# Shorter Sinkhorn rounds, a second pass all in Strassen products, and the last pass's x split earlier

## The chip, the core and the metric

The kernel runs on one core of a Trainium2 chip. The metric is the device time of one launch in microseconds. Five engines work side by side, each with a queue of its own that it takes in order: TensorE (PE, matmuls), VectorE (DVE), ScalarE (ACT), GpSimd (POOL) and SyncE (SP), which issues most DMA transfers. An engine waits for another by a semaphore, and what stands behind a waiting instruction waits too.

## What is computed

Three stages follow each other on 2304 tokens of width 512:

```
attn  = softmax(q k^T / 8) v          # in chunks of 64, 8 heads
P     = exp(x w_gate - max)           # x: attn as [2304, 512], 8 experts
repeat 8 times:
    P /= P.sum(1) + 1e-9              # rows: over the experts
    P /= P.sum(0) + 1e-9              # columns: over the tokens
    P *= N / E
out   = sum over e of P[:, e] * (relu(x w1[e]) w2[e])       # hidden width 1024
y     = LN(h * softmax(h)) w_out,  h = out w_in             # per token
```

All is float32. A product is made of three matmuls of rounded parts: each operand is split into a high part (rounded by ScalarE) and a low part (the rest, a subtraction on VectorE or POOL), and high*high, high*low and low*high are added up in PSUM.

## The kernel before

The tokens are taken in three passes of 768, each as two halves of 384. In every pass the 32 units (8 experts by 4 quarters of the hidden width) are gone through; `unit(m)` gives pass and unit of the m-th of 96 visits. In visit m the loop does the first layer of unit m and the second layer of an earlier unit, so PE alternates between groups of six matmuls of the one and of the other.

The first layer of a unit (`l1`) is one two-by-two Strassen step: seven products of six matmuls, 42 in all, into the PSUM banks X, Y and Z; VectorE forms the four blocks of h from them. For this x is kept as seven blocks (`XOPS`: B11, B21, B22 and the sums T1 to T4), each with high and low part. The blocks of the second and the third pass are made while the first pass runs, or shortly after it (`x_steps`, queued in `late` and `late2`), written to DRAM (`x_kept`) and loaded when their pass begins.

The second layer has two forms. In the plain one (`l2`) a unit has eight parts (half, output block pair, block) of six matmuls, 48 in all, with four weight blocks A11 to A22. In the Strassen one (`l2s`) two units are taken together: seven products (`SECOND`) of two parts of six matmuls, 84 for the pair, with seven weight blocks a unit; h needs sums T1 to T4 as well (`h_sums`, on POOL), and the seven accumulators are put together at the pass's end (`l2s_sums`). The weight sums S1 to S4 come from `second_sums`.

Which form a visit has is set by M2: visits below M2 are plain. The first pass is plain throughout. The second takes the ten units of `PLAIN` first, in plain form, and then the 22 of `EARLY`, whose sums were made in the first pass; `acc_change` turns the plain accumulators into Strassen ones there. The sums of the ten are made on POOL in the second pass, for the third, which is Strassen throughout.

The Sinkhorn rounds run as side steps in the first units of the first pass: `run_side(k)` takes k steps, once after each first-layer product and once after each second-layer part. A round is one matmul with a matrix of ones, which sums over the tokens on the partitions (`sink_sum`), the column step (`sink_cols`) and the row step (`sink_rows`) on VectorE, and an idle step. Its result must be written out and read back as `share` tiles before unit 4 scales h by it.

The rest of the order is set by `events[7 * n + i]`, functions due at product i of visit n, by two queues of weight steps (`w_side`) and of last-stage weights (`prep`), and by the pools: tiles of a tag share a fixed number of buffers (15 for x and h blocks, tag `six`; 18 for weight blocks, tag `w`), so a load can wait until a buffer comes free. SP's queue is one: a store that waits for POOL holds up the loads issued behind it.

Of the kernel before, what the change touches and what calls it, by code (L numbers as in the profile page):

```python
# [44 lines left out]
def chunk_attention_sinkhorn_moe_solu_kernel(  # L45
# [14 lines left out]
    P = 128  # L60
# [25 lines left out]
    EARLY = [u for u in range(NU) if u not in PLAIN]  # L86
    ORDER = [list(range(NU)), PLAIN + EARLY, list(range(NU))]
    NM = NPASS * NU
    M2 = NU + len(PLAIN)

# [47 lines left out]
    ident = const.tile([P, P], F32, name="ident")  # L138
    ones = const.tile([P, P], F32, name="ones")
    mhalf = const.tile([P, 1], F32, name="mhalf")  # L140
# [3 lines left out]
    lg = const.tile([P, NT, E], F32, name="lg")  # L144
    pw_e = const.tile([P, E, NT], F32, name="pw")
    pw = pw_e.rearrange("p e t -> p t e")

# [204 lines left out]
    def gate(t):  # L352
# [10 lines left out]
        nc.vector.tensor_copy(lg[:, t, :], pg[:, :E])  # L363

    def sink_start():
# [11 lines left out]
    def sink_exp(pm):  # L377
        nm = small.tile([P, 1], F32, tag="m1", name="nm")
        nc.vector.tensor_reduce(out=nm, in_=pm[:, :P], axis=AX.X, op=ALU.max)
        nc.vector.tensor_scalar(  # L380
            out=lg, in0=lg, scalar1=nm, scalar2=None, op0=ALU.subtract
        )
        nc.scalar.activation(out=pw, in_=lg, func=AF.Exp)

    def sink_rows(pc):
        r = pc[:, 256:256 + NT]
        nc.vector.tensor_reduce(out=r, in_=pw, axis=AX.X, op=ALU.add)
        nc.vector.tensor_scalar(out=r, in0=r, scalar1=EPS, scalar2=None, op0=ALU.add)
        nc.vector.reciprocal(out=r, in_=r)
        nc.vector.tensor_tensor(  # L390
            out=pw, in0=pw, in1=r.unsqueeze(2).to_broadcast([P, NT, E]), op=ALU.mult
        )

    def sink_sum():
        pc = spare("pc")
        nc.tensor.matmul(
            pc[:, :NT * E], ones, pw_e.rearrange("p e t -> p (e t)"), start=True, stop=True
        )
        return pc

    def sink_cols(pc):
        r = pc[:, 192:192 + E]
        nc.vector.tensor_reduce(
            out=r, in_=pc[:, :NT * E].rearrange("p (e t) -> p e t", e=E), axis=AX.X, op=ALU.add
        )
        nc.vector.tensor_scalar(out=r, in0=r, scalar1=EPS, scalar2=None, op0=ALU.add)
        nc.vector.reciprocal(out=r, in_=r)
        nc.vector.scalar_tensor_tensor(
            out=pw,
            in0=pw,  # L410
            scalar=float(N) / E,
            in1=r.unsqueeze(1).to_broadcast([P, NT, E]),
            op0=ALU.mult,
            op1=ALU.mult,
        )
# [32 lines left out]
    def sink_steps():  # L448
        def start():
            sink["mb"] = sink_start()  # L450

        def first():
            sink["pm"] = sink_max(sink["mb"])

        def expo():
            sink_exp(sink["pm"])
            sink_rows(sink["pm"])

        def summed():
            sink["pc"] = sink_sum()  # L460

        def cols():
            sink_cols(sink["pc"])

        def rows():
            sink_rows(sink["pc"])

        def shares():
            load_share(0)
            load_share(1)  # L470

        idle = lambda: None
        steps = [start, first, expo, idle]
        for i in range(8):
            steps += [summed, cols, rows, idle]
        return steps[:-2] + [sink_out, shares]
# [84 lines left out]
    def second_blocks(u):  # L561

        def block(n):
            def go():
                t = wtile([P, 2, 256], F32R, f"w2_{u}_{n}")
                split(t[:, 0], t[:, 1], w2_block(u, n), nc.gpsimd)
                wo2[u, n] = t
                if n != "A21" or u in PLAIN:
# [300 lines left out]

    def acc_change(p):  # L870


        at = {w: n for n, (w, _) in enumerate(SECOND)}
        for w, j, d in (("A12", 0, 0), ("A22", 0, 2), ("S4", 1, 0), ("S1", 1, 2)):
            acc[p, at[w]] = acc[p, j, d]
        a, b = acc[p, at["S4"]], acc[p, at["S1"]]
        nc.vector.tensor_tensor(out=a, in0=a, in1=b, op=ALU.subtract)

    def l2s_sums(p):
# [204 lines left out]
    with tc.manual_schedule():  # L1084
# [3 lines left out]
        for i in range(WARM):  # L1088
            nc.tensor.transpose(warm[:, :P], ident, ident)
        nc.gpsimd.memset(ones, 1.0)  # L1090
        nc.gpsimd.memset(mhalf, -0.5)
# [83 lines left out]

        late = deque(x_steps(1, nc.vector))
        late2 = deque(x_steps(2, nc.gpsimd))
        prep.extend(
# [18 lines left out]
        event(7 * (M2 + 1), lambda: acc_change(1))  # L1197
        for m in range(M2, NM):
            for g, f in h_sums(m, nc.vector if m == NM - 1 else nc.gpsimd):
                event(g, f)  # L1200
            if m % 2 == 0:
                for n, (wn, _) in enumerate(SECOND):
                    for q_ in range(2):
                        event(7 * (m + 2) + 2 * n - 5,
                              lambda u=unit(m + q_)[1], wn=wn: w_load(u, wn, 1))
            if m % NU == 0:
                for i in range(6):
                    event(7 * (m + 2) + i,
                          lambda i=i, p=m // NU - 1: l2s_sums(p)[i]())
        for n in range(NM):  # L1210
# [35 lines left out]
            for i in range(7):  # L1246
# [38 lines left out]
        for k in range(14):  # L1285
# [3 lines left out]
            if k == 7:  # L1289
                mlp_b(0)  # L1290
                mlp_a(2)
        assert not events and not late2
        load_out(0, 15)
# [51 lines left out]
```

## Time and profile before

| | us |
|---|---|
| median of 3 runs | 1798.76 (1795.76 to 1800.87) |
| the profiled execution | 1800.11 |
| its span, first to last instruction | 1798.3 |
| PE busy in it | 1758.6 (98%) |
| VectorE, POOL, ScalarE busy | 1371.6, 1022.1, 615.1 |
| granted TensorE clock, mean | 0.991 of full speed |

The span falls into the attention (to about 110 us, with the first unit at its end), the first pass (to about 626), the second pass (to about 1090), the third (to about 1575) and the last stage, per tile of 128 tokens. Reading it: an engine's busy time counts its instructions alone, a wait is put down to the engine and line that came last, and the span is that of the instructions, 1.8 us less than the whole execution.

### The profile page before, as it was taken

The page shows a single profiled execution, that of the slowest core. Times are in us where ns is not written, and L with a number is a line of the kernel's source. Part 1 is how long each engine was busy: PE and PEld are TensorE (multiplying, and loading weights), DVE is VectorE, ACT ScalarE, POOL GpSimd, SP SyncE. Part 2 cuts the span into 40 slices and gives each one's busy share as a digit, 9 for nine tenths or more (in the row PEclk, how much of TensorE's full clock was granted, in tenths as well). Part 3 has the DMA queues.
Part 4 walks back from the last instruction along what each step waited for, and adds up shares of the span by engine and source line. Part 5 has one row for each costly group of instructions (what it writes and reads, how often), then busy time and mean ns, then how long its engine had stood idle before and what let it go on. Part 6 is the DMA issues. An engine that isn't in the chain of part 4 may idle for free. (4 is left out here: it accounts for less than half of the span.)

```text
span 1798.3 us, 32046 instructions
## 1 busy us (share of the span) xinstructions
PE 1758.6 (98%) x10869; PEld 1705.0 (95%) x10869; DVE 1371.6 (76%) x2271; ACT 615.1 (34%) x1394; POOL 1022.1 (57%) x1132
## 2 busy tenths in 40 slices
PE   7989999999999999999999999999999999999999
PEld 6878999999999999999999999999999999988887
DVE  6767888889887757778787878888877877766664
ACT  6733444444444312223333332223232232222222
POOL 2656888888888411148878776656566655400000
PEclk9899999999999999999999999999999999999999
DMA  7766898898899998879999999888888888931110
GB/s 186 187 217 205 292 330 310 306 336 296 310 314 333 356 337 282 252 250 320 345 320 313 332 340 394 299 275 263 289 283 287 276 267 258 301 132 65 56 48 30
DMA packets 297154, 476.20 MB, mean 265 GB/s; under 512 B 47760, under 2 KB 100128, under 8 KB 296992
## 3 DMA queue, kind: packets, MB, share of 16 engines
q1 hardware_dynamic: 296272, 470.23, 77.3%
q10 hardware_dynamic: 720, 3.93, 0.5%
q8 instruction: 87, 1.43, 0.3%
q14 instruction: 75, 0.61, 0.1%
HBM read 325.08 MB, written 148.97 MB: 264 GB/s over the span
## 5 line engine op out<-in xcount | busy, mean ns | idle before, releaser
L673 POOL TENSOR_TENSOR ho_T<-hT,ho_T 128x384 fp32r<-128x384 f32 x212 | 230.3, 1088 | 165.4 <-ACT ho_T L672 143.7
L796 PE MATMUL y<-h,w_A 128*128 128x384 f32 x1536 | 303.0, 334 | 0.0
L796 PEld LDWEIGHTS y<-h,w_A 128*128 128x128 f32 x1536 | 269.2, 188 | 0.0
L751 DVE TENSOR_TENSOR t<-Y,s 128x384 f32<-128x384 f32 x192 | 106.2, 553 | 155.0 <-PE Y L653 117.4
L151 POOL TENSOR_TENSOR w_A<-raw,w_A 128x256 fp32r<-128x256 f32 x224 | 168.9, 766 | 97.3 <-ACT w_A L150 97.3
L672 ACT ACTIVATE ho_B<-hp 128x384 fp32r<-128x384 f32 x162 | 85.2, 526 | 354.8 <-DVE hp L706 348.7
L847 PE MATMUL y<-ho_T,wl_S 128*128 128x384 f32 x972 | 195.1, 335 | 0.2 <-DVE acc L867 0.2
L867 DVE TENSOR_TENSOR acc<-y,acc 128x768 f32<-128x768 f32 (+1 forms) x186 | 170.4, 919 | 19.5 <-PE y L847 19.4
L847 PEld LDWEIGHTS y<-ho_T,wl_S 128*128 128x128 f32 x972 | 171.5, 189 | 1.0 <-DVE acc L867 0.5
L681 POOL TENSOR_TENSOR hT<-hp,hp 128x384 f32<-128x384 f32 x106 | 113.3, 1090 | 92.2 <-DVE hp L706 82.5
L823 DVE TENSOR_TENSOR acc<-y,acc 128x768 f32<-128x768 f32 (+1 forms) x168 | 153.1, 912 | 8.3 <-PE y L796 6.7
L653 PE MATMUL X<-x_B,wl_A 128*128 128x384 f32 x768 | 154.7, 336 | 2.1 <-ACT s L755 2.1
L653 PE MATMUL Y<-x_T,wl_S 128*128 128x384 f32 x768 | 154.8, 336 | 0.0
L672 ACT ACTIVATE ho_T<-hT 128x384 fp32r<-128x384 f32 x216 | 111.3, 516 | 107.2 <-POOL hT L681 102.6
L653 PEld LDWEIGHTS X<-x_B,wl_A 128*128 128x128 f32 x768 | 135.8, 189 | 2.4 <-ACT s L755 2.4
L653 PEld LDWEIGHTS Y<-x_T,wl_S 128*128 128x128 f32 x768 | 135.8, 189 | 0.4 <-DVE hp L706 0.3
L847 PE MATMUL y<-ho_B,wl_A 128*128 128x384 f32 x648 | 130.0, 336 | 0.0
L1044 POOL TENSOR_TENSOR r<-r,mhalf 128x1 f32<-128x1 f32 x18 | 9.9, 549 | 208.5 <-DVE r L1041 208.5
L673 DVE TENSOR_TENSOR ho_B<-hp,ho_B 128x384 fp32r<-128x384 f32 x162 | 122.8, 758 | 2.9 <-ACT ho_B L672 2.5
L681 POOL TENSOR_TENSOR hT<-hp,hT 128x384 f32<-128x384 f32 x106 | 122.4, 1155 | 0.1
L847 PEld LDWEIGHTS y<-ho_B,wl_A 128*128 128x128 f32 x648 | 114.7, 189 | 0.0
L727 ACT ACTIVATE h<-X 128x384 fp32r<-128x384 f32 x76 | 37.4, 492 | 203.3 <-DVE X L723 174.1
(173 smaller groups left out, 3725.1 us busy)
## 6 DMA issues: line engine op xcount, KB each, us to landing
wl_S<-wk SPq DMA_DIRECT2D x472, 256.0 KB, 4.6
wl_A<-wk SPq DMA_DIRECT2D x394, 256.0 KB, 4.7
wk<-w_S SPq DMA_DIRECT2D x256, 256.0 KB, 3.4
wk<-w_A SPq DMA_DIRECT2D x202, 256.0 KB, 3.1
raw<-in_moe_w_dram SPq DMA_DIRECT2D x71, 512.0 KB, 5.8
sh<-spread SPq DMA_DIRECT2D x64, 192.0 KB, 5.5
kept<-wp SPq DMA_DIRECT2D x32, 256.0 KB, 4.1
xk_T<-x_T SPq DMA_DIRECT2D x8, 768.0 KB, 4.3
```

Of the source, the lines that this page charges most:

```text
L151: (eng or nc.vector).tensor_tensor(out=lo, in0=src, in1=hi.bitcast(F32), op=ALU.subtract)
L653: nc.tensor.matmul(b, w[:, a, kk, :], x[:, c, kk, :], start=(first and kk == 0 and n == 0), stop=(kk == 1 and n == 2), skip_group_check=no ...
L672: nc.scalar.activation(out=hi, in_=x, func=AF.Copy)
L673: f = lambda: eng.tensor_tensor(out=lo, in0=x, in1=hi.bitcast(F32), op=ALU.subtract)
L681: eng.tensor_tensor(out=hb[m, n], in0=hb[m, a], in1=hb[m, b], op=ALU.subtract)
L727: nc.scalar.activation(out=hi, in_=hp, func=AF.Copy)
L751: nc.vector.tensor_tensor(out=c_of[n], in0=bank_, in1=c_of[other], op=ALU.add)
L796: nc.tensor.matmul(y, wo2[u, f"A{d // 2 + 1}{f + 1}"][:, a, i * P:(i + 1) * P], h[:, c, f, :], start=(f == 0 and n == 0), stop=(f == 1 and ...
L823: nc.vector.tensor_tensor(out=at, in0=y, in1=at, op=ALU.add)
L847: nc.tensor.matmul(y, wo2[unit(m + q_)[1], wn][:, a, i * P:(i + 1) * P], hop[m // 2, bn][:, q_, c, :], start=(q_ == 0 and o == 0), stop=(q ...
L867: nc.vector.tensor_tensor(out=at, in0=y, in1=at, op=ALU.add)
L1044: nc.gpsimd.tensor_tensor(out=r2, in0=r2, in1=mhalf, op=ALU.pow)
```

## The change

Sinkhorn: `pw` gets one column more per token tile, filled with EPS, and one tile row more, filled with EPS / 128, and the matrix of ones becomes one of E / N. So the sums come out with EPS added and scaled, and the additions of EPS, the scaling by N / E and the subtraction of the maximum go (the last becomes the bias of the exponential). Column and row step become one side step, with two idle ones behind; the side steps of visit 1 are taken one at a time. The last column step writes `pw_e`, in the old layout.

Second pass: `ORDER[1]` takes `EARLY` first and `PLAIN` last, and M2 is 32, so the whole pass is in Strassen form. `acc_change` and the loads and stores of plain blocks for the second pass go, and the sums of the ten `PLAIN` units are made from visit 35 on instead of 37. The eight plain parts of the last first-pass unit are spread over visits 32 and 33, four in each.

x: the eighteen steps for the third pass move from visits 31 to 37, on POOL, to the first pass, on VectorE, behind those for the second pass. The queue of both now gets one step in a unit of `EARLY` too, from unit 5 on.

```diff
-    ORDER = [list(range(NU)), PLAIN + EARLY, list(range(NU))]
+    ORDER = [list(range(NU)), EARLY + PLAIN, list(range(NU))]
-    M2 = NU + len(PLAIN)
+    M2 = NU
...
-    ones = const.tile([P, P], F32, name="ones")
+    ratio = const.tile([P, P], F32, name="ratio")
-    pw_e = const.tile([P, E, NT], F32, name="pw")
-    pw = pw_e.rearrange("p e t -> p t e")
+    pw_x = const.tile([P, NT + 1, E + 1], F32, name="pw")
+    pw = pw_x[:, :NT, :E]
+    pw_e = const.tile([P, E, NT], F32, name="pw_e")
...
-        nc.vector.tensor_reduce(out=r, in_=pw, axis=AX.X, op=ALU.add)
-        nc.vector.tensor_scalar(out=r, in0=r, scalar1=EPS, scalar2=None, op0=ALU.add)
+        nc.vector.tensor_reduce(out=r, in_=pw_x[:, :NT, :], axis=AX.X, op=ALU.add)
...
-            out=r, in_=pc[:, :NT * E].rearrange("p (e t) -> p e t", e=E), axis=AX.X, op=ALU.add
-        )
-        nc.vector.tensor_scalar(out=r, in0=r, scalar1=EPS, scalar2=None, op0=ALU.add)
+            out=r,
+            in_=pc[:, :SC].rearrange("p (t e) -> p e t", e=E + 1)[:, :E, :],
+            axis=AX.X,
+            op=ALU.add,
+        )
...
-            steps += [summed, cols, rows, idle]
+            steps += [summed, lambda i=i: cols(i == 7), idle, idle]
...
-        late = deque(x_steps(1, nc.vector))
-        late2 = deque(x_steps(2, nc.gpsimd))
+        late = deque(x_steps(1, nc.vector) + x_steps(2, nc.vector))
...
-        for m in range(NU, M2):
-            u = unit(m)[1]
-            for k, wn in enumerate(("A11", "A12", "A21", "A22")):
-                event(7 * m + 2 + k, lambda u=u, wn=wn: w_load(u, wn, 1))
-            g = 7 * (NU + 5) + 18 * (m - NU)
+        for n, u in enumerate(PLAIN):
+            g = 7 * (NU + 3) + 18 * n
...
-                    run_side(2 if n == 1 and i < 4 else 1)
+                    run_side(1)
-                if NU > n > NQ and n in PLAIN and i in (1, 2, 4, 6) and late:
+                if NU > n > NQ and i in ((1, 2, 4, 6) if n in PLAIN else (2,)) and late:
                     late.popleft()()
-                if n > NU - 2 and i in (1, 3, 5) and late2:
-                    late2.popleft()()
...
-                if 0 < n <= M2:
-                    for part in parts[i:i + 1] if i < 6 else parts[6:]:
-                        l2(n - 1, *part, apart=apart)
+                if 0 < n <= M2 + 1:
+                    if n < M2:
+                        todo = parts[i:i + 1] if i < 6 else parts[6:]
+                    else:
+                        k = i // 2 + 4 * (n - M2)
+                        todo = parts[k:k + 1] if i % 2 == 0 else []
+                    for part in todo:
+                        l2(min(n, M2) - 1, *part, apart=apart)
```

What this does to the queues shows at three places. On PE, at the first Sinkhorn sum in visit 1 (X and Y are first-layer products, y second-layer parts, pm the maximum, pc the column sums), before:

```order
L653 MATMUL X_1872<-x_B_688,w_A_1554 128x384 x6
L374 MATMUL pm<-ident,mb 128x128
L796 MATMUL y_0_0_0_1895<-h_0_1714,w_0_A_1638 128x384 x3
L796 MATMUL y_0_0_0_1895<-h_0_1714,w_0_A_1642 128x384 x3
L653 MATMUL Y_1915<-x_T_1144,w_S_1696 128x384 x6
L396 MATMUL pc<-pw,ones 128x144
L796 MATMUL y_0_0_1_1934<-h_0_1714,w_0_A_1638 128x384 x3
L796 MATMUL y_0_0_1_1934<-h_0_1714,w_0_A_1642 128x384 x3
L653 MATMUL X_1872<-x_B_775,w_A_1634 128x384 x6
```

and now:

```order
L794 MATMUL y_0_0_0_1895<-h_0_1717,w_0_A_1641 128x384 x3
L794 MATMUL y_0_0_0_1895<-h_0_1717,w_0_A_1645 128x384 x3
L377 MATMUL pm<-ident,mb 128x128
L651 MATMUL Y_1909<-x_T_1147,w_S_1699 128x384 x6
L794 MATMUL y_0_0_1_1932<-h_0_1717,w_0_A_1641 128x384 x3
L794 MATMUL y_0_0_1_1932<-h_0_1717,w_0_A_1645 128x384 x3
L651 MATMUL X_1874<-x_B_778,w_A_1637 128x384 x6
L395 MATMUL pc<-pw,ratio 128x171
```

`pm` now has a second-layer part ahead of it, and between `pm` and the first `pc` stand three groups of six matmuls instead of two.

On VectorE, one round in visit 2 (pc holds the sums and their reciprocals, pw the matrix, acc the second layer's accumulator), before:

```order
L751 TENSOR_TENSOR t_2219<-Y_2145,s_2123 128x384
L403 TENSOR_REDUCE pc<-pc 128x8
L406 TENSOR_SCALAR pc<-pc 128x8
L407 RECIPROCAL pc<-pc 128x8
L408 SCALAR_TENSOR_TENSOR pw<-pw,pc 128x18x8
L823 TENSOR_TENSOR acc_1_0_1977<-y_1_0_1_2237,acc_1_0_1977 128x384
L387 TENSOR_REDUCE pc<-pw 128x18
L388 TENSOR_SCALAR pc<-pc 128x18
L389 RECIPROCAL pc<-pc 128x18
L390 TENSOR_TENSOR pw<-pw,pc 128x18x8
```

and now:

```order
L749 TENSOR_TENSOR c_2265<-Y_2128,s_2106 128x384
L402 TENSOR_REDUCE pc<-pc 128x8
L408 RECIPROCAL pc<-pc 128x8
L409 TENSOR_TENSOR pw<-pw,pc 128x18x8
L387 TENSOR_REDUCE pc<-pw 128x18
L388 RECIPROCAL pc<-pc 128x18
L389 TENSOR_TENSOR pw<-pw,pc 128x18x8
```

The two additions are gone, and the row step follows the column step with nothing of the layers between.

On SP, at the change from the first pass to the second (wl: weight blocks loaded, first the unit, then the block, then 0 for the first layer and 1 for the second; wk: weights stored; xk: blocks of x stored; ak: accumulators stored), the issues of visit 32 before:

```order
L621 DMA wl1_S3_0_8102<-wk1_95 128x512
L556 DMA wk30_124<-w2_30_S1_7943 128x512
L621 DMA wl1_S1_0_8122<-wk1_95 128x512
L310 DMA xk2_B21_88<-x2_B21_8045 128x1536
L829 DMA ak0_0_126<-acc0_0_0_1902 128x768
L621 DMA wl1_A22_0_8143<-wk1_95 128x512
L621 DMA wl0_A11_1_8145<-wk0_94 128x512
L556 DMA wk30_124<-w2_30_S2_7997 128x512
L621 DMA wl1_S4_0_8164<-wk1_95 128x512
L621 DMA wl0_A12_1_8168<-wk0_94 128x512
L829 DMA ak0_1_127<-acc0_1_0_1977 128x768
L621 DMA wl0_A21_1_8189<-wk0_94 128x512
```

and those of visit 33 now:

```order
L827 DMA ak0_1_128<-acc0_1_0_1969 128x768
L619 DMA wl5_A11_0_8212<-wk5_100 128x512
L619 DMA wl5_S2_0_8214<-wk5_100 128x512
L619 DMA wl5_A12_0_8216<-wk5_100 128x512
L619 DMA wl5_S3_0_8227<-wk5_100 128x512
L619 DMA wl5_S1_0_8249<-wk5_100 128x512
L619 DMA wl5_A22_0_8265<-wk5_100 128x512
L619 DMA wl2_A11_1_8267<-wk2_97 128x512
L619 DMA wl3_A11_1_8269<-wk3_98 128x512
L827 DMA ak0_0_127<-acc0_0_2_2033 128x768
L619 DMA wl5_S4_0_8288<-wk5_100 128x512
L619 DMA wl2_A12_1_8306<-wk2_97 128x512
```

Before, the store of x block B21 for the third pass stood ahead of the loads for the next unit and of the plain blocks of unit 0; now no store of x is left here, and the first second-layer loads are those of the pair of units 2 and 3, behind one unit's first-layer blocks.

## Rows read from the trace of the kernel before

**Rows 1.** The page's busy times: engine, us busy, share, instructions.

```profile
PE 1758.6 (98%) x10869; PEld 1705.0 (95%) x10869; DVE 1371.6 (76%) x2271; ACT 615.1 (34%) x1394; POOL 1022.1 (57%) x1132
```

**Rows 2.** Busy times by stage: stretch, length, each engine's us (instructions), clock, DMA share, GB/s.

```profile
core 0: us, PE busy (x) PEld busy (x) DVE busy (x) ACT busy (x) POOL busy (x), PEclk, DMA share, GB/s
112.80:157.30 44.50, 34.49 (x191) 31.96 (x192) 35.46 (x99) 12.68 (x35) 23.81 (x33) 1.00 0.55 196
...
180.00:600.00 420.00, 420.00 (x2425) 420.00 (x2424) 353.11 (x574) 189.15 (x516) 348.18 (x458) 1.00 0.89 313
...
626.50:638.70 12.20, 9.42 (x38) 8.65 (x37) 3.60 (x5) 1.05 (x3) 0.00 (x0) 0.72 1.03 393
...
788.50:807.50 19.00, 15.89 (x80) 14.93 (x79) 12.55 (x21) 6.14 (x14) 16.25 (x17) 0.91 0.60 183
807.50:1120.00 312.50, 311.78 (x1797) 311.07 (x1797) 246.54 (x377) 96.50 (x207) 241.48 (x237) 1.00 0.96 338
1120.00:1143.00 23.00, 20.39 (x108) 19.89 (x107) 22.79 (x29) 5.19 (x11) 12.69 (x10) 0.93 0.71 253
```

**Rows 3.** PE's waits, whole span: waiter, for whom, us in total, times, longest.

```profile
PE pc L396 <- DVE pw L390: 8.7, 8, 2.0
...
PE Z L653 <- DVE X L751: 4.3, 3, 2.6
...
PE y L796 <- DMA wl_A<-wk: 2.8, 2, 2.0
PE X L653 <- ACT s L755: 2.1, 1, 2.1
...
PE pm L374 <- DVE mb L369: 1.3, 1, 1.3
...
PE pwt L426 <- DVE pw L408: 0.7, 1, 0.7
```

**Rows 4.** Timeline of PE, a Sinkhorn round: start, us, instruction, idle before.

```profile
139.46 0.51 PE L396 MATMUL pc<-pw,ones 128*128 128x144 f32 x2 [0.88 <-DVE pw L390]
139.71 1.30 PE L653 MATMUL Y<-x_T,w_S 128*128 128x384 f32 x6
...
144.62 0.51 PE L396 MATMUL pc<-pw,ones 128*128 128x144 f32 x2 [0.49 <-DVE pw L390]
```

**Rows 5.** Timeline of VectorE in the same round.

```profile
141.59 0.30 DVE L403 TENSOR_REDUCE pc<-pc 128x8 f32<-128x144 f32 x1
141.93 0.17 DVE L406 TENSOR_SCALAR pc<-pc 128x8 f32<-128x8 f32 x1
142.14 0.22 DVE L407 RECIPROCAL pc<-pc 128x8 f32<-128x8 f32 x1
...
142.72 0.55 DVE L823 TENSOR_TENSOR acc<-y,acc 128x384 f32<-128x384 f32 x1
143.19 0.41 DVE L387 TENSOR_REDUCE pc<-pw 128x18 f32<-128x144 f32 x1
143.63 0.18 DVE L388 TENSOR_SCALAR pc<-pc 128x18 f32<-128x18 f32 x1
143.85 0.28 DVE L389 RECIPROCAL pc<-pc 128x18 f32<-128x18 f32 x1
144.16 0.41 DVE L390 TENSOR_TENSOR pw<-pw,pc 128x144 f32<-128x144 f32 x1
```

**Rows 6.** Waits of SP's queue between 560 and 700 us.

```profile
SPq L310 <- POOL x_T L308: 11.4, 4, 3.4
```

**Rows 7.** The x split: times, then duration in ns, least, median, most.

```profile
L304 ACT ACTIVATE x_B<-xf x9: 835/843/848, 38.6 to 617.3; 128x768 fp32r<-128x768 f32 x9
...
L308 DVE TENSOR_TENSOR x_B<-xf,x_B x3: 948/1341/1403, 242.4 to 304.8; 128x768 fp32r<-128x768 f32 x3
...
L308 DVE TENSOR_TENSOR x_T<-xs_T,x_T x4: 947/1164/1405, 367.2 to 492.0; 128x768 fp32r<-128x768 f32 x4
...
L339 DVE TENSOR_TENSOR xs_T<-xf,xs_T x2: 947/983/1019, 315.8 to 427.7; 128x768 f32<-128x768 f32 x2
```

More of the change, by code (lines that the diff above doesn't have):

```diff
@@ L363, in gate @@
         nc.vector.tensor_copy(lg[:, t, :], pg[:, :E])
+    SC = (NT + 1) * (E + 1)
     def sink_start():
@@ L378, in sink_exp @@
         nm = small.tile([P, 1], F32, tag="m1", name="nm")
-        nc.vector.tensor_reduce(out=nm, in_=pm[:, :P], axis=AX.X, op=ALU.max)
-        nc.vector.tensor_scalar(
-            out=lg, in0=lg, scalar1=nm, scalar2=None, op0=ALU.subtract
-        )
-        nc.scalar.activation(out=pw, in_=lg, func=AF.Exp)
+        nc.vector.tensor_reduce(out=nm, in_=pm[:, :P], axis=AX.X, op=ALU.max, negate=True)
+        nc.scalar.activation(out=pw, in_=lg, func=AF.Exp, bias=nm, scale=1.0)
     def sink_rows(pc):
         r = pc[:, 256:256 + NT]
-        nc.vector.tensor_reduce(out=r, in_=pw, axis=AX.X, op=ALU.add)
-        nc.vector.tensor_scalar(out=r, in0=r, scalar1=EPS, scalar2=None, op0=ALU.add)
+        nc.vector.tensor_reduce(out=r, in_=pw_x[:, :NT, :], axis=AX.X, op=ALU.add)
         nc.vector.reciprocal(out=r, in_=r)
@@ L396, in sink_sum, with sink_cols @@
         nc.tensor.matmul(
-            pc[:, :NT * E], ones, pw_e.rearrange("p e t -> p (e t)"), start=True, stop=True
+            pc[:, :SC], ratio, pw_x.rearrange("p t e -> p (t e)"), start=True, stop=True
         )
         return pc
-    def sink_cols(pc):
+    def sink_cols(pc, last):
         r = pc[:, 192:192 + E]
         nc.vector.tensor_reduce(
-            out=r, in_=pc[:, :NT * E].rearrange("p (e t) -> p e t", e=E), axis=AX.X, op=ALU.add
+            out=r,
+            in_=pc[:, :SC].rearrange("p (t e) -> p e t", e=E + 1)[:, :E, :],
+            axis=AX.X,
+            op=ALU.add,
         )
-        nc.vector.tensor_scalar(out=r, in0=r, scalar1=EPS, scalar2=None, op0=ALU.add)
         nc.vector.reciprocal(out=r, in_=r)
-        nc.vector.scalar_tensor_tensor(
-            out=pw,
+        nc.vector.tensor_tensor(
+            out=pw_e.rearrange("p e t -> p t e") if last else pw,
             in0=pw,
-            scalar=float(N) / E,
             in1=r.unsqueeze(1).to_broadcast([P, NT, E]),
-            op0=ALU.mult,
-            op1=ALU.mult,
+            op=ALU.mult,
         )
@@ L460, in summed, with cols @@
             sink["pc"] = sink_sum()
[L462 to L466, printed above, removed]
+        def cols(last):
+            sink_cols(sink["pc"], last)
+            if not last:
+                sink_rows(sink["pc"])
         def shares():
@@ L567, in go @@
                 wo2[u, n] = t
-                if n != "A21" or u in PLAIN:
+                if n != "A21":
                     w_keep(u, n, True, t)
@@ L868, in l2s @@
         flush()
[L870 to L877, printed above, removed]
     def l2s_sums(p):
@@ L1089, in chunk_attention_sinkhorn_moe_solu_kernel @@
             nc.tensor.transpose(warm[:, :P], ident, ident)
-        nc.gpsimd.memset(ones, 1.0)
+        nc.gpsimd.memset(ratio, float(E) / N)
+        nc.gpsimd.memset(pw_x, EPS)
+        nc.gpsimd.memset(pw_x[:, NT, :], EPS / P)
         nc.gpsimd.memset(mhalf, -0.5)
@@ L1196, in chunk_attention_sinkhorn_moe_solu_kernel @@
                 event(g + 7 + k, f[k])
-        event(7 * (M2 + 1), lambda: acc_change(1))
         for m in range(M2, NM):
@@ L1205, in chunk_attention_sinkhorn_moe_solu_kernel @@
                               lambda u=unit(m + q_)[1], wn=wn: w_load(u, wn, 1))
-            if m % NU == 0:
+            if m == 2 * NU:
                 for i in range(6):
@@ L1291, in chunk_attention_sinkhorn_moe_solu_kernel @@
                 mlp_a(2)
-        assert not events and not late2
+        assert not events
         load_out(0, 15)
```

## Prediction

> **What bounds the kernel now.** I read the page's head first. PE is busy 1758.6 us, 98% of the span [rows 1]; a matmul that goes, or a wait of PE that goes, is time unless something else takes its place. Next the table by stage [rows 2]. From 180 to 600 us PE never idles: 2425 matmuls of 384 columns in 420.0 us, 0.1732 us each, and that pitch is my unit. The other stages differ by what PE lost: the stretch 112.8 to 157.3 (the Sinkhorn rounds), 626.5 to 638.7 (the first pass's end), 788.5 to 807.5 (where the second layer turns from plain to Strassen), 1120 to 1143 (early in the last pass). Then PE's waits [rows 3]. They name the same places: 8.7 us in eight waits of the column sums `pc` for the row step, 1.3 and 0.7 us for `pm` and `pwt` beside them, 2.8 us for a weight load, 2.1 us for ScalarE, and 4.3 us of Z waiting for VectorE. Last I read one Sinkhorn round on both engines [rows 4, 5], and SyncE's queue around 626 us [rows 6].
>
> **Matmuls removed.** A plain unit has 48 second-layer matmuls, a Strassen unit 42 (84 for a pair). Ten units change: 60 matmuls less, all of 384 columns, each at PE's own pitch. 60 x 0.1732 = 10.4 us. In the plain second-pass stretch PE has no wait of its own that could hide this.
>
> **Sinkhorn rounds.** The waits there sum to 8.7 + 1.3 + 0.7 = 10.7 us [rows 3]. In the round shown the sums start at 139.46 and the next at 144.62, 0.49 us of that waiting [rows 4]. VectorE comes to the columns at 141.59 (it first needs PE's next product) and ends the rows at 144.56 [rows 5]. The change takes out two additions (0.21 us from 141.93 to 142.14, 0.22 from 143.63 to 143.85) and the accumulation that stood between columns and rows (0.47, from 142.72 to 143.19): 0.90 us. The rows then end 4.2 us after the sum. PE has four groups of six matmuls (4.16 us) and the sum itself (about 0.25) between two sums, so this wait goes. The first rounds had three groups between sums, and now all have four, since the double step in the first unit is gone; that is worth up to 1.04 us to each of them. I leave 0.3 us for `pm` (one group now stands ahead of it), 0.7 for the first sum (three groups ahead of it, and the exponential in its chain), 0.5 for `pwt`, and 1.0 over the other rounds: 2.5 left of 10.7. The sum is 171 columns wide instead of 144, about 0.05 us each, 0.4 in all. Net gain 7.8 us. Bounds: 4.5, if every round still waits 0.7, and 10.
>
> The new column reduction reads PSUM with a step of nine elements, where the old one read it straight in about 0.3 us; no row has a strided reduction from PSUM. The nearest, the rows' strided reduction from SBUF, starts 0.44 us before the next operation [rows 5], 0.1 more than the columns' 0.34. I take 0.1 a round, within the 1.0 above.
>
> **The ends of passes.** The stretch of 12.2 us at 626.5 holds 38 matmuls, which need 6.6: 5.6 lost, partly to the two weight waits and partly to the clock, 0.72 granted on average, so much of it at the 1.2 GHz level. Those loads are the plain second-layer blocks of unit 0, late because SyncE's queue, which is in order, held them behind stores of the last pass's x that waited 11.4 us for POOL [rows 6]. Both the loads and those stores are gone from there. What is late next: the pair loads of the first Strassen products, issued during visit 33 and wanted at visit 34; visit 33 has 66 matmuls, 11.4 us, since it also holds half of the last plain unit. The transfers can move 393 GB/s there [rows 2]. The stretch of 19.0 us at 788.5 holds 80 matmuls, which need 13.9: 5.1 lost. It has a unit with first-layer matmuls alone (42, or 7.3 us), while POOL is busy 16.25 of 19 us with new sums and h blocks; VectorE and ScalarE wait for POOL and PE for them. The new turn has two units of 66 matmuls, and POOL's sums start only two units later. I take back 1.5 us of the 10.7 for the new turn: gain 9.2. Bounds: 4, if the new turn loses as much as the costlier of the old ones and a little more, and 10.7. The loss at 1120 to 1143 (23.0 us for 108 matmuls, or 4.3) is the accumulators' sums in the last pass; its steps stand where they did, and I leave it.
>
> **The x split in the first pass.** Seven low parts and four differences now run on VectorE between units 5 and 25: 3 x 1.34 + 4 x 1.16 + 4 x 0.98 = 12.6 us, and seven high parts of 0.84 us on ScalarE [rows 7]. From 180 to 600 VectorE is idle 420 - 353.1 = 66.9 us and ScalarE 230.9 [rows 2], some 2.5 us of VectorE in a unit of 15.6; a unit with weight sums gets one step (at most 1.4 us), the others four. Cover is there: cost 0, bounds 0 and 10. It uses buffers that h also needs, which can hold ScalarE for a matmul group or two, as the steps for the second pass do already with no PE wait in this stretch.
>
> **Ten more Strassen units.** Between 807.5 and 1120 such units ran with POOL busy 241.5 of 312.5 us, the DMA engines 96%, and 0.7 us lost in 21.5 units (1797 matmuls over 84). Ten more with the same load, and one more with half a plain unit, cost 0.4; the shares (two tiles of 192 KB a visit) come in eight visits over the last ten units instead of over 22, 0.17 MB more a unit or 12 GB/s: about 350 instead of 338. Bounds 0 and 8.
>
> **Sum.** -10.4 - 7.8 - 9.2 + 0.4 = -27.0. The profiled execution took 1800.1 us in all (1798.3 of span), which gives 1773.1. The median of the runs is 1798.8, 1.3 lower, so the same sum from there gives 1771.8. I forecast 1773.
>
> **Rivals.**
>
> *The new turn stalls.* It joins two changes of stage in one place: x of the next pass, the accumulators' stores and the first pair loads come together. For it: both old turns lost 5 us each, and the stores wait in order on SyncE ahead of the loads. Against: fewer stores, no POOL wait in the queue. If it loses 9 us instead of 1.5: 1780 to 1781. Chance 0.12.
>
> *Sinkhorn does not get shorter.* If PE's wait is set by VectorE's own queue (accumulations and h parts ahead of the columns), only the two additions (0.4 x 8 = 3.4) are gained: 1773 + 4.4 = 1777 to 1778, and with a slow strided reduction (0.3 more a round) 1780. Chance 0.08.
>
> *The second pass is paced by transfers or POOL.* For it: 96% of the DMA engines' time. Against: the same units ran at PE's pitch, and 393 GB/s were moved at 626.5 [rows 2]. If each of 30 units lost 0.5 us: 1788. Chance 0.09. The Trainium skill, DMA: Bandwidth & Descriptors, Specifications, gives about 358 GB/s of HBM for a core, which would leave 2% above 350; this trace moved 393 for 12 us, so the trace does not hold to that figure.
>
> *Slower: the first pass is paced by the moved split.* One mechanism, in units 5 to 25: VectorE's eleven steps (12.6 us) find no idle time in the units that also make weight sums, and each of the seven high parts waits on ScalarE for an h buffer for two groups (2.1 us) plus its own 0.84 us: 12.6 + 20.6 = 33 us, 1806. It decides against the change once more than 27 us of it reach PE. Against it: 66.9 us idle on VectorE there, steps of at most 1.4 us against 2.5 a unit. For it: the x rows vary from 0.95 to 1.40 us, so something holds them. Chance 0.05. The Trainium skill, SBUF — State Buffer, Who interferes with whom, says that a VectorE instruction with two SBUF inputs contends with a GpSimd instruction that reads SBUF, and that whichever starts second is blocked to the other's end. The spread of those rows agrees. By that rule POOL, which makes the weights of the first pass and is busy 348.2 of 420 us, could lose the same 12.6 us; if its late weights held PE for all of it the sum would be 14.4 and the time 1786, but POOL's idle 71.8 us stand against that.
>
> **How the numbers follow.** Forecast case 0.66, its own range 1767 to 1780 (all gains at their best -31, so 1769 from the profiled time and 1768 from the median; Sinkhorn at 4.5 and turn at 7 together 1779). The others as above. The range 1766 to 1788 takes in the two rivals near 1780, most of the third, and leaves the slower one and a part of the third out, near 1 in 10, and as much for what I don't see. 0.3% is 5.4 us, about what a measurement of this kernel tells from no change: faster means below 1793.4. Faster holds in the first four cases almost whole, 0.94; same 0.02; slower 0.04.
>
> **What would show it.** Right: PE's count 60 lower; `pc` waits summing to some 2 us instead of 8.7; no weight wait and a full granted clock where the first pass ends, and no second low stretch 150 us later; first pass from 180 us on with PE full. Wrong: PE waits for X or Z in units 5 to 25, or for `wl` loads from visit 33 on; `pc` waits of 0.5 us or more in every round; POOL above 90% in the second pass with PE waiting for `ho`.

## The result and the profile after

The changed kernel takes 1772.27 us (median of 4 runs, 1771.00 to 1774.52) against 1798.04 for the kernel before (4 runs): ratio 0.9857, 95% interval 0.9839 to 0.9875. The forecast was 1773, between 1766 and 1788. The profiled execution took 1771.9, with a span of 1770.1.

The page's head, which answers to [rows 1]:

```profile
PE 1742.8 (98%) x10809; PEld 1689.2 (95%) x10809; DVE 1372.1 (78%) x2249; ACT 631.2 (36%) x1424; POOL 1094.4 (62%) x1203
```

PE has 60 matmuls less. Its waits (us in total, times, longest), to set beside [rows 3]:

```profile
PE Z L651 <- DVE X L749: 4.2, 3, 2.6
...
PE pc L395 <- DVE pw L389: 1.3, 3, 0.6
...
PE y L845 <- DMA wl_A<-wk: 0.6, 1, 0.6
PE y L794 <- DVE acc L821: 0.6, 2, 0.4
PE y L845 <- DMA wl_S<-wk: 0.5, 2, 0.3
PE pwt L425 <- DVE pw_e L409: 0.5, 1, 0.5
...
PE pm L377 <- DVE mb L372: 0.3, 1, 0.3
```

The column sums wait 1.3 us instead of 8.7, `pm` and `pwt` 0.8 instead of 2.0. The wait for ScalarE and most of that for `wl_A` are gone, and the Z products wait as before. By stage, with the columns of [rows 2]:

```profile
109.40:162.60 53.20, 51.10 (x291) 49.22 (x290) 43.87 (x111) 20.33 (x55) 37.86 (x51) 1.00 0.63 220
180.00:600.00 420.00, 419.42 (x2418) 418.57 (x2417) 361.90 (x583) 192.81 (x518) 352.46 (x452) 1.00 0.91 324
600.60:623.50 22.90, 22.90 (x134) 22.90 (x133) 16.64 (x29) 5.28 (x11) 6.24 (x6) 1.00 0.97 341
623.50:1064.60 441.10, 438.55 (x2523) 436.54 (x2522) 343.81 (x529) 134.01 (x290) 330.92 (x329) 1.00 0.94 330
1064.60:1128.20 63.60, 60.78 (x338) 59.59 (x337) 54.86 (x78) 17.63 (x36) 37.83 (x34) 0.97 0.91 332
```

The third row is the first pass's turn: no idle PE and a full clock, where [rows 2] had 12.2 us with 38 matmuls at 0.72. The last two rows are where time is still lost: PE is idle for 2.6 us of the one and 2.8 of the other.

To compare kernels I cut each trace at the same instruction, the first X product of a visit, so that a stage covers the same visits in each (us between those starts, each from the one profiled execution of its kernel):

| visits | before | changed | difference | what it is |
|---|---|---|---|---|
| start to 1 | 111.57 | 109.38 | -2.2 | attention, unchanged code |
| 1 to 4 | 62.52 | 53.18 | -9.3 | Sinkhorn rounds |
| 4 to 32 | 436.80 | 438.08 | +1.3 | first pass |
| 32 to 34 | 37.17 | 22.88 | -14.3 | 48 matmuls less (8.3), and 6.0 of losses |
| 34 to 64 | 445.45 | 441.04 | -4.4 | 12 matmuls less (2.1), and losses |
| 64 to 68 | 63.06 | 63.63 | +0.6 | accumulators' sums |
| 68 to 95 | 393.12 | 393.12 | 0.0 | third pass, at PE's pitch |
| 95 to the end | 248.6 | 248.8 | +0.2 | last stage |

One Sinkhorn round on PE in the kernel after (start, us, instruction), to set beside [rows 4]:

```profile
138.92 0.45 PE L395 MATMUL pc<-pw,ratio 128*128 128x171 f32 x2
139.10 1.34 PE L651 MATMUL Y<-x_T,w_A 128*128 128x384 f32 x6
...
143.40 0.45 PE L395 MATMUL pc<-pw,ratio 128*128 128x171 f32 x2
```

and the chain between the two on VectorE, to set beside [rows 5]:

```profile
141.08 0.31 DVE L402 TENSOR_REDUCE pc<-pc 128x8 f32<-128x152 f32 x1
141.42 0.22 DVE L408 RECIPROCAL pc<-pc 128x8 f32<-128x8 f32 x1
141.67 0.30 DVE L409 TENSOR_TENSOR pw<-pw,pc 128x144 f32<-128x144 f32 x1
142.01 0.33 DVE L387 TENSOR_REDUCE pc<-pw 128x18 f32<-128x162 f32 x1
142.38 0.28 DVE L388 RECIPROCAL pc<-pc 128x18 f32<-128x18 f32 x1
142.69 0.31 DVE L389 TENSOR_TENSOR pw<-pw,pc 128x144 f32<-128x144 f32 x1
```

Columns and rows take 1.92 us in one piece (141.08 to 143.00), where they took 2.98 with an accumulation between them. The sum at 143.40 finds its operand ready.

### The profile page after: what moved, and what is told of

The parts are those of the page before. It is cut to its first block, busy times and chain, and to the rows that moved or that the text cites. A ratio compares the mean times of both kernels' runs of the same rounds, so it can differ in the third digit from the quotient of the medians.

```text
span 1770.1 us, 32103 instructions
## 1 busy us (share of the span) xinstructions
PE 1742.8 (98%) x10809; PEld 1689.2 (95%) x10809; DVE 1372.1 (78%) x2249; ACT 631.2 (36%) x1424; POOL 1094.4 (62%) x1203
## 5 line engine op out<-in xcount | busy, mean ns | idle before, releaser
L671 POOL TENSOR_TENSOR ho_T<-hT,ho_T 128x384 fp32r<-128x384 f32 x252 | 276.1, 1097 | 196.0 <-ACT ho_T L670 178.3
L845 PE MATMUL y<-ho_T,wl_S 128*128 128x384 f32 x1152 | 231.5, 336 | 0.6 <-DMA wl_S<-wk 0.5
L845 PEld LDWEIGHTS y<-ho_T,wl_S 128*128 128x128 f32 x1152 | 203.0, 188 | 2.0 <-PE Z L651 1.1
L679 POOL TENSOR_TENSOR hT<-hp,hp 128x384 f32<-128x384 f32 x126 | 133.4, 1080 | 98.4 <-DVE hp L704 90.0
L670 ACT ACTIVATE ho_T<-hT 128x384 fp32r<-128x384 f32 x256 | 131.7, 516 | 124.9 <-POOL hT L679 120.2
L845 PE MATMUL y<-ho_B,wl_A 128*128 128x384 f32 x768 | 153.5, 334 | 0.6 <-DMA wl_A<-wk 0.6
L671 DVE TENSOR_TENSOR ho_B<-hp,ho_B 128x384 fp32r<-128x384 f32 x192 | 143.9, 750 | 3.8 <-ACT ho_B L670 3.2
L679 POOL TENSOR_TENSOR hT<-hp,hT 128x384 f32<-128x384 f32 x126 | 143.4, 1138 | 0.0
L845 PEld LDWEIGHTS y<-ho_B,wl_A 128*128 128x128 f32 x768 | 134.8, 188 | 1.1 <-DVE acc L865 0.9
L152 POOL TENSOR_TENSOR w_S<-ws,w_S 128x256 fp32r<-128x256 f32 x128 | 102.8, 820 | 7.6 <-ACT w_S L151 7.6
```

What stands on the lines that cost most here:

```text
L152: (eng or nc.vector).tensor_tensor(out=lo, in0=src, in1=hi.bitcast(F32), op=ALU.subtract)
L670: nc.scalar.activation(out=hi, in_=x, func=AF.Copy)
L671: f = lambda: eng.tensor_tensor(out=lo, in0=x, in1=hi.bitcast(F32), op=ALU.subtract)
L679: eng.tensor_tensor(out=hb[m, n], in0=hb[m, a], in1=hb[m, b], op=ALU.subtract)
L845: nc.tensor.matmul(y, wo2[unit(m + q_)[1], wn][:, a, i * P:(i + 1) * P], hop[m // 2, bn][:, q_, c, :], start=(q_ == 0 and o == 0), stop=(q ...
```

## The experiments

"Visits 1 to 4" and the like are the stages of the table above. Each kernel was timed beside runs of the kernel before on its chip, and times are compared by their ratio to it.

**One part alone: Sinkhorn.** The edit is the Sinkhorn part of the diff, on the kernel before.

```diff
+    pw_x = const.tile([P, NT + 1, E + 1], F32, name="pw")
+            steps += [summed, lambda i=i: cols(i == 7), idle, idle]
+                    run_side(1)
```

> The kernel before with the Sinkhorn part of the change alone (EPS and E/N folded into the sums, column and row step in one, one side step at a time in visit 1). My theory, from the waits that the change leaves in the profile after (2.1 of 10.7 us): 8 to 9.5 us shorter than before, about 1789. Rival, only the two additions a round count (0.4 us x 8): 3.4 shorter, about 1794.6. Rival, the change pays only together with the new order of the second pass: no difference.

1788.32 us, ratio 0.9945 (0.9932 to 0.9957): 9.4 less than before's 1797.74. Visits 1 to 4 take 53.18, as in the changed kernel, and all other stages are within 0.8 of before. Neither rival holds.

**One part alone: the x split.**

```diff
-        late = deque(x_steps(1, nc.vector))
-        late2 = deque(x_steps(2, nc.gpsimd))
+        late = deque(x_steps(1, nc.vector) + x_steps(2, nc.vector))
```

> The kernel before with the third pass's x split in the first pass on VectorE alone; second pass and Sinkhorn as before. My theory: the stores that waited 11.4 us for POOL leave SyncE's queue at the first pass's end, the plain weight loads of unit 0 come in time and most of the 5.6 us lost there come back, while the first pass pays at most 1.3: 2.5 to 5 us shorter than before, 1793 to 1795.5. Rival, the loss there is set by the turn itself (stores of the accumulators, loads of x): no difference, or 1 us longer. Rival of the prediction, the split paces the first pass: 5 us longer or more.

1795.32 us (11 runs), ratio 0.9985 (0.9977 to 0.9994), 2.4 less, 1.1 to 4.1 by the interval. The trace has both terms: visits 32 to 34 take 31.20 instead of 37.17, which is the pitch of their 180 matmuls, and visits 4 to 32 take 437.97, 1.2 more. Visits 32 to 34 by windows in this kernel:

```profile
611.20:642.40 31.20, 31.20 (x182) 31.20 (x181) 21.69 (x36) 4.70 (x10) 0.00 (x0) 1.00 1.04 383
```

The two terms make 4.8 less between the two traces, twice what the medians show. The profiled execution of before, at 1800.1, stood 2.4 above the median of this batch, so a part of the 6.0 lost in it at visit 33 may be its own, and the size is open between the two. That the loss is gone is plain, with the plain weight loads of unit 0 still there, so the x split caused it, whatever form the second pass has. SyncE's waits of 11.4 us for POOL's x blocks are gone from its queue, and POOL is idle in this stretch; that the loss came through the waiting stores is read from that queue and from PE's weight waits there.

**The changed kernel with the old rounds.** The Sinkhorn part of the diff undone, with the two steps at a time in visit 1.

> The changed kernel with the old Sinkhorn rounds (its second pass and its x split stay). If the parts add up, as I think: 8 to 9.5 us longer than the changed kernel, 1780 to 1782. Rival, the two parts share a gain (the clock, or work that shifts into the first units): 5 us or less longer. If the waits of before come back, the column sums wait about 8 to 9 us in all again.

1783.48 us, ratio 0.9919 (0.9905 to 0.9932), against 0.9857, or 0.9866 when repeated, with the new rounds: 9.5 to 11 us of 1798. The column sums wait 8.8 us again and visits 1 to 4 take 62.57, 9.4 more; the rest is in the attention (1.1 more) and in visits 64 to 68 (65.07, 1.4 more), stages that vary between kernels in which they are alike. The parts add up.

**The last plain unit not spread.**

```diff
-                if 0 < n <= M2 + 1:
-                    if n < M2:
+                if 0 < n <= M2:
+                    if True:
```

> The changed kernel with all eight plain second-layer parts of the first pass's last unit in visit 32, as a unit of the first pass has them, and the first layer alone in visit 33. My theory was that the halves in visits 32 and 33 give the pair loads time: without them visit 33 has 42 matmuls (7.3 us) ahead of the first Strassen products, and 2 to 5 us are lost there, 1774.5 to 1777.5. Rival, the losses at the old turns came from POOL (weight sums and h blocks, 16.25 of 19 us) and from stores that waited for it, and both are away from here now: no difference, 1772 to 1773.

1774.83 us, ratio 0.9870 (0.9856 to 0.9883). PE's timeline where the first Strassen products begin, in this kernel:

```profile
623.57 1.21 PE L651 MATMUL X<-x_B,wl_A 128*128 128x384 f32 x6
626.05 0.77 PE L845 MATMUL y<-ho_B,wl_A 128*128 128x384 f32 x3 [1.28 <-DMA wl_A<-wk]
627.79 0.76 PE L845 MATMUL y<-ho_B,wl_A 128*128 128x384 f32 x3 [0.97 <-DMA wl_A<-wk]
628.39 2.06 PE L651 MATMUL Y<-x_T,wl_S 128*128 128x384 f32 x6
```

The same stretch by windows, in this kernel

```profile
623.50:638.00 14.50, 12.25 (x61) 11.66 (x60) 7.06 (x12) 3.60 (x8) 8.93 (x10) 0.88 1.05 391
```

and in the changed one:

```profile
623.50:638.00 14.50, 14.50 (x86) 14.50 (x85) 10.03 (x16) 4.96 (x11) 10.19 (x10) 1.00 1.03 382
```

Without the halves PE waits 2.25 us for the pair weights, the clock is 0.88 of full speed on average, and fewer matmuls are done: 61 matmuls instead of 86, about 4.3 us, and visits 34 to 64 take 445.35 instead of 441.04. By the ratios the kernel is 2.3 us longer than the changed one, or 0.7 longer than its repetition (below, 0.9866), so the time does not decide between theory and rival; that the loads come late, and that visits 34 to 64 lose by it, is in the rows.

**Two side steps at a time in visit 1.**

```diff
-                    run_side(1)
+                    run_side(2 if n == 1 and i < 4 else 1)
```

> The changed kernel with two side steps at a time in the first products of visit 1, as the kernel before has them, so that the first rounds have three groups of matmuls (3.1 us) between sums instead of four. A round's chain on VectorE is about 4.2 us. If the chain sets the first rounds: each of the two or three rounds concerned waits about 1 us, but starts as much earlier, so the sum is within 1 us of the changed kernel. If the slots set the time and not the chain: no wait, no difference. In no case more than 2 us.

1775.49 us, ratio 0.9877 (0.9860 to 0.9895). I expected 2 us at most, and visits 1 to 4 take 57.10, 3.9 more. PE's waits there (us in total, times, longest):

```profile
PE pc L395 <- DVE pw L389: 2.4, 4, 1.3
PE pwt L425 <- DVE pw_e L409: 1.8, 1, 1.8
PE pm L377 <- DVE mb L372: 1.3, 1, 1.3
```

That is 5.5 against 2.1: 1.1 more for the column sums, 1.0 for `pm`, which again has no second-layer part ahead of it, and 1.3 for `pwt`. By the ratios the whole kernel is 2.0 to 3.6 us longer. My expectation forgot what PE is here: a chain that ends earlier gives nothing back to an engine that has matmuls waiting in any case, so each wait that the tighter spacing makes is lost.

**The additions put back.**

```diff
         nc.vector.tensor_reduce(out=r, in_=pw_x[:, :NT, :], axis=AX.X, op=ALU.add)
+        nc.vector.tensor_scalar(out=r, in0=r, scalar1=0.0, scalar2=None, op0=ALU.add)
```

and the same in the column step.

> The changed kernel with two additions a round put back at their old places (of 0.0, so the values stay); columns and rows stay one side step. The chain grows by 0.43 us a round, eight rounds. If taking out the additions is what made the waits go: 2 to 3.5 us longer than the changed kernel. Rival, merging column and row step is what did it (in the round of before VectorE came to the columns only with PE's next product, and an accumulation of 0.47 us stood between columns and rows), and there is slack left: 0 to 1 us longer, with the column sums waiting under 3 us in all.

1774.68 us, ratio 0.9868 (0.9850 to 0.9886). Visits 1 to 4 take 55.72, 2.5 more, and the column sums wait 2.7 us in five waits. The ratios give only 0.4 to 2.0 more, less than their intervals tell apart, so the stage decides. It lies between the two theories: the additions are worth 2.5 of the 9.3, the single steps in visit 1 by the run above 3.9. What is left, near 3, is for the merged step and the folded subtraction and scaling, if the three are independent, which no run shows.

**The third pass's x on POOL.**

```diff
-        late = deque(x_steps(1, nc.vector) + x_steps(2, nc.vector))
+        late = deque(x_steps(1, nc.vector) + x_steps(2, nc.gpsimd))
```

> The changed kernel with the third pass's x split in the first pass on POOL instead of VectorE. POOL was busy 348 to 352 of 420 us there with the weights' low parts; eleven steps more, up to 2 us each, find 68 us idle. Theory, both engines have cover: within 1.5 us of the changed kernel. Rival, the split delays weights that PE needs, since POOL is the engine with less room in units with weight sums: 3 us longer or more, with PE waiting for weight blocks between 250 and 600 us.

1773.35 us, ratio 0.9863 (0.9844 to 0.9882), no difference. The first pass in this kernel:

```profile
180.00:600.00 420.00, 419.43 (x2418) 418.61 (x2417) 351.18 (x572) 192.57 (x518) 365.06 (x463) 1.00 0.91 324
```

The third pass's arithmetic takes 12.6 us on POOL (365.06 against 352.46) where it took 10.7 on VectorE (361.90 against 351.18), and costs PE nothing on either: it runs from visit 16 on, and PE's two waits of 0.6 us in all, in visits 7 and 9 as in the changed kernel, come earlier. Visits 4 to 32 take 438.08 in both. About those early waits the run says nothing, since the steps in the visits up to 12 are the second pass's, and VectorE makes their low parts in this kernel too:

```profile
200.12 0.95 DVE L309 TENSOR_TENSOR x_B<-xf,x_B 128x768 fp32r<-128x768 f32 x1
```

**The accumulators' sums spread.** Seven additions (the text below counts nine) in six steps of visit 66 become seven steps of one addition each, from visit 64 on.

```diff
+                (4, lambda: (add("A12", "A11"), keep(p, 0, 0, t["A12"]))),
+                (10, lambda: add("S4", "S1")),
+                (12, lambda: add("S2", "A11")),
...
+                for i, at in enumerate((4, 10, 12, 13, 14, 15, 17)):
+                    event(7 * m + at, lambda i=i: l2s_sums(1)[i][1]())
```

> The changed kernel with the accumulators' sums at the second pass's end in another order: nine additions, taken one at a time from visit 64 on as their operands are done, instead of in six steps in visit 66. In the changed kernel the Z product of 1109.85 us waits 2.61 us for VectorE behind those additions (1.75 us each), and the stretch 1085 to 1110 holds 22.4 us of matmuls in 25. If the bunch of additions is what holds the product: 2.5 to 4.4 us shorter than the changed kernel, about 1768 to 1770. Rival, VectorE has no room there at all and the additions only hold something else: no difference.

1769.56 us, ratio 0.9843 (0.9825 to 0.9861). The Z product of that place in the changed kernel

```profile
1109.85 1.54 PE L651 MATMUL Z<-x_B,wl_S 128*128 128x384 f32 x6 [2.61 <-DVE X L749]
```

and in this one:

```profile
1110.65 1.31 PE L651 MATMUL Z<-x_B,wl_S 128*128 128x384 f32 x6 [1.63 <-DVE X L749]
```

Visits 64 to 68 take 61.69 instead of 63.63. In the eight traces here with the sums as in the changed kernel the stage takes 62.6 to 65.1, so the gain is at least 0.9 us. The bunch was part of it, and 1.6 us of wait stay.

**The changed kernel again.**

> The changed kernel itself, unaltered, timed beside the three that follow. Expected as before: 1771 to 1774. In the trace the attention's end differs by up to 2 us between executions of kernels that are alike there (108.8 to 112.3 us over the runs so far); if the 2.2 us by which it was earlier in the changed kernel is that, it moves again, while the stretch from the first product of visit 1 to that of visit 4 stays at 53.2 us, visits 4 to 32 at 438.1 and visits 32 and 33 at 22.9.

1773.86 us, ratio 0.9866 (0.9849 to 0.9882). The attention ends at 111.88, 2.5 later than in the first profile, while the three stages named repeat: 53.17, 438.04 and 22.88. Visits 64 to 68 take 62.81, 0.8 less, and the last stage 249.6, 0.8 more. So the 2.2 us of the first row of the table are within what executions of one kernel differ by.

**Sums spread, and no weight preparation beside them.**

```diff
-                if n > NU + 2 and i in (1, 3, 5) and prep:
+                if n > NU + 2 and n not in (64, 65, 66) and i in (1, 3, 5) and prep:
```

> The kernel with the accumulators' sums at the second pass's end spread out, and besides no preparation of last-stage weights on VectorE in visits 64 to 66. With the sums spread, VectorE is still without a gap from 1095 to 1106 us and a Z product waits 1.63 us there; four of those steps (3.2 us) stand among the additions. If VectorE's load is what holds the product: visits 64 to 67 take 58.3 to 60 us instead of 61.7 (63.6 in the changed kernel), 2 us less in all, 1767 to 1768. Rival, the spread additions are too late for the next unit in any case: no difference to them alone.

1768.07 us, ratio 0.9839 (0.9824 to 0.9853). The stretch of the additions by windows, in this kernel

```profile
1085.00:1110.00 25.00, 24.92 (x144) 24.60 (x143) 23.95 (x33) 6.77 (x14) 15.22 (x12) 1.00 0.75 269
1110.00:1115.00 5.00, 5.00 (x31) 5.00 (x30) 4.47 (x7) 1.44 (x3) 1.98 (x2) 1.00 1.06 402
```

and in the changed one:

```profile
1085.00:1110.00 25.00, 22.39 (x129) 21.90 (x128) 23.93 (x31) 5.19 (x11) 13.99 (x11) 1.00 0.86 310
1110.00:1115.00 5.00, 5.00 (x20) 5.00 (x21) 5.00 (x8) 1.62 (x4) 1.01 (x1) 0.66 0.55 182
```

VectorE's load held the product: visits 64 to 68 take 59.51 (their 336 matmuls need 58.2), and the low clock behind the wait (0.66, now 1.00) goes with it. The preparation comes later at no cost, as visits 68 to 95 still take 393.12.

**The x steps' start.**

```diff
-                if NU > n > NQ and i in ((1, 2, 4, 6) if n in PLAIN else (2,)) and late:
+                if NU > n > NQ and i in ((1, 2, 4, 6) if n in PLAIN else (2,) if n > 12 else ()) and late:
```

> The changed kernel with the step of the x split in a unit of EARLY only from visit 13 on (four in each unit of PLAIN as before). Visits 7, 9 and 12 are 0.42, 0.65 and 0.14 us longer than their matmuls need in the changed kernel, and with the split on POOL just as much, which speaks for the buffers shared with h (ScalarE waited 3.49 us for one at 206.8) and not for VectorE's time. If these early steps are it: visits 4 to 32 take 436.8 to 437.2 instead of 438.1, about 1 us less. Rival, the same steps cost the same later: no difference, with losses in visits 13 to 25.

1770.57 us, ratio 0.9853 (0.9839 to 0.9868). The first pass in this kernel:

```profile
180.00:600.00 420.00, 420.00 (x2424) 419.99 (x2423) 363.00 (x585) 192.02 (x518) 351.65 (x452) 1.00 0.90 324
```

Visits 4 to 32 take 436.85, as before the change, with the same steps taken later: it was the early ones. What the expectation draws from the run with x on POOL does not follow, as said there; that the buffers are the cause, and not VectorE's time, is shown by neither run.

**All three.** The two edits above and the spread sums.

> The changed kernel with the spread sums, the pause in visits 64 to 66 and the x split's early steps moved behind visit 12. If the three add up: 2 + 2 + 1 us less than the changed kernel, 1767 to 1768, the third pass at PE's pitch as before. Rival, the weights' preparation that was put off comes back in the third pass as a wait: the gain of the pause is lost there.

1768.21 us, ratio 0.9837 (0.9822 to 0.9851), 5.7 us below the changed kernel beside it. Each gain is in the trace (436.87, 58.66, 393.12), but the third edit does not show in the median beside 1768.07 without it.

## Why the prediction was right, step by step

**Matmuls removed: right.** 10869 became 10809; 10.4 us by the pitch, in visits 32 to 34 and 34 to 64.

**Sinkhorn rounds: right in mechanism, larger in size.** 9.3 against 7.8. The waits left are 2.1 us instead of the 2.5 I left. The wider sum, charged at 0.4, cost nothing: the matmuls behind it start 0.17 to 0.28 us after it (0.18 in the round shown), 1.89 in all eight, where they started 0.25 after the old one each time [rows 4], 2.04 in all. The strided reduction from PSUM, which I had no row for, takes 0.315 us (median of eight), 0.01 more than the old one. The new layout of `pw` did more than I saw: the row reduction, now over neighbours in SBUF, takes 0.33 us instead of 0.41 though it is 18 elements longer, and the row step's product 0.31 instead of 0.41 [rows 5]. Waits gone (8.6 us) and stage (9.3) leave 0.7 that I can't assign. The single steps of visit 1, which I named only as up to 1.04 us a round, are the largest piece that a run shows apart.

**The ends of passes: right, and I held back too much.** 6.0 came back at visit 33 and 5.5 at visits 43 and 44 (27.36 us in the trace of before, for 126 matmuls that need 21.84), where I had read 5.6 and 5.1; the new turn lost nothing, where I charged 1.5. What I said of the cause stands for the first part, which the x split alone brought back. For the second part the rows of before agree (VectorE waits 2.77 and 3.19 us for POOL's part of h at 798.63 and 805.82), but no run takes POOL's work alone away. SyncE's queue after the change, between 560 and 700 us (us in total, times, longest), to set beside [rows 6]:

```profile
SPq L827 <- DVE acc L821: 5.4, 2, 3.1
SPq L554 <- POOL w_A L152: 4.7, 4, 2.1
...
SPq L554 <- DMA x_B<-xk_B: 4.0, 1, 4.0
```

No store of x waits for POOL there. Among the rows of stores that of the accumulators is now the longest, which is what the first rival named (the rows of loads, up to 7.7 us, are waits for a free buffer). With the eight parts in one visit the rival's stall is there, at some 4 us of its 9, and the spread keeps it away. Which of these three waits makes the loads late in that kernel no run shows.

**The x split: cost 0 forecast, 1.3 measured.** The term that was missed is the second pass's x. I priced the third pass's steps as the only new ones in units 5 to 25. But both passes' steps are in one queue, which now starts at unit 5: the second pass's ran in visits 8 to 24 before and run in visits 5 to 16 now, and the third pass's follow, in visits 16 to 25. The loss is in visits 7, 9 and 12 (0.42, 0.65 and 0.14 us), beside the second pass's steps. From visit 13 on nothing is lost, so for the steps that I priced "cover is there" held. Two rows of ScalarE in the kernel after, in visits 6 and 8:

```profile
206.76 0.49 ACT L725 ACTIVATE h<-X 128x384 fp32r<-128x384 f32 x1 [3.49 <-PE y L794]
```

```profile
237.50 0.85 ACT L305 ACTIVATE x_B<-xf 128x768 fp32r<-128x768 f32 x1 [3.00 <-DMA xk_B<-x_B]
```

It waits until PE or a store has done with a buffer, and its h is late. VectorE waits 1.33 us for that h at 207.29, its accumulation of 209.65 comes behind it, and PE waits for that at 210.74 (0.17 us; 0.41 at 242.66). From 180 to 320 us ScalarE's h waits for PE to be done with a buffer for 16.1 us in five waits, against 8.2 in two before and 11.7 in three with the early steps moved. That the early steps cause the loss is shown by the run that moves them; that it comes through the buffers is read from these rows alone, and that VectorE's own load in these visits causes it, since it takes the low parts there, is a rival that no run takes away. So the slower rival's wait of ScalarE for a buffer is in the rows, and the first pass lost 1.3 us of its 33. The split itself became faster, VectorE's rows in the first pass, which answer to [rows 7] (times, then duration in ns, least, median, most):

```profile
L309 DVE TENSOR_TENSOR x_B<-xf,x_B x6: 948/994/1326, 200.4 to 403.7; 128x768 fp32r<-128x768 f32 x6
```

**Ten more Strassen units: 0.4 forecast, about 3.3 measured.** Visits 34 to 64 have 2520 matmuls, 436.7 us at 0.1733, and took 441.04: 4.3 lost, against about 1.0 outside the turn before. The named waits are Z for VectorE (0.68 and 0.93 us) and two loads of pair weights (0.63 and 0.31), which the prediction had named as a sign of being wrong. That lies within the bound of 8, but the term was mis-sized: a stretch with 0.7 us of loss in 21.5 units did not show what the others would do. The kernels that are alike in this stage lost 3.9 to 4.8, and the one with x on POOL 6.8; what sets this was not tried. The transfers did not set a pace: 330 GB/s over the stage, where I estimated 350, and 382 for 14.5 us without a PE wait. The Trainium skill, DMA: Bandwidth & Descriptors, Specifications, gives a limit of about 358 for a core; the second figure is above it.

**What I did not forecast** is 2.2 us of the attention and the 0.8 of the last stages, the first of which moves between executions of one kernel. The terms as measured, -10.4 - 9.3 - 11.5 + 1.3 + 3.3 - 2.2 + 0.8 = -28.0, agree with the spans' -28.2. The medians show 25.8: the profiled execution of before stood 2.1 above its median and that of the change 0.4 below. Which terms are larger in that execution of before than in a middle one, no trace shows. So the sum of -27.0 came out near partly by luck: gains too small by 2.3 (turns) and 1.5 (Sinkhorn) stood against costs too small by 1.3 and 2.9.

## What to carry to other kernels

Where an engine is busy to the end, a dependent chain beside it is free as long as the engine has enough other work between the chain's steps. Here the chain's steps taken one at a time in the first visit, with more matmuls between them, were worth 3.9 us and two additions less in each round 2.5; ending the chain earlier was worth nothing. When a transfer is late, look for a store ahead of it in the same queue that waits for an engine; here moving the work behind that store brought the load in time. Before a step is called covered, check each queue that it enters, the buffers that it takes and what else moves with it: here the steps that were priced cost nothing, and those that they pushed forward did.

## What the runs showed of the hardware

The additions of accumulators, all of one shape, take 0.94 to 1.76 us in the kernel with sums spread and preparation paused. The seven after 1577 us, where POOL is idle, take 0.95 each. VectorE at the second pass's end (start, us):

```profile
1093.00 0.95 DVE L873 TENSOR_TENSOR acc<-acc,acc 128x768 f32<-128x768 f32 x1
...
1103.48 1.76 DVE L873 TENSOR_TENSOR acc<-acc,acc 128x768 f32<-128x768 f32 x1
```

and POOL in it:

```profile
1094.13 1.01 POOL L671 TENSOR_TENSOR ho_T<-hT,ho_T 128x384 fp32r<-128x384 f32 x1 [5.40 <-PE y L845]
...
1103.10 1.32 POOL L671 TENSOR_TENSOR ho_T<-hT,ho_T 128x384 fp32r<-128x384 f32 x1
1104.38 1.73 POOL L679 TENSOR_TENSOR hT<-hp,hT 128x384 f32<-128x384 f32 x1
```

The first runs while POOL is idle. The second starts 0.38 us after POOL's instruction, which ends at 1104.42, and ends at 1105.24, 0.82 later, about as if it had begun only then; POOL's next, from 1104.38, takes 1.73 instead of some 1.0 to 1.3. The Trainium skill, SBUF — State Buffer, Who interferes with whom, says that a VectorE instruction with two SBUF inputs and a GpSimd instruction that reads SBUF exclude each other, and the later one waits to the other's end; these rows agree. So the additions at a pass's end took up to 1.9 times their own time beside POOL's sums of h.
